# Two 32-head attentions with a gate on one core: the last head joined to the last tile of the output projection, and the first segment's projection units moved to other steps

## The chip, the cores and the metric

The kernel runs on one core of one Trainium2 chip. A core has five engines with a queue each: PE (TensorE, matrix products; its weight loads are listed as PEld), DVE (VectorE), ACT (ScalarE), POOL (GpSimd) and SP (SyncE, which here only issues DMAs). Matmuls write to PSUM; DVE and ACT read it. The metric is the device time of one execution in microseconds (us), lower is better. The kernel before took 2798.84, 2795.10 and 2796.87 us in three runs; the median is 2796.87 us.

## What is computed

Two multi-head attentions over the same 2048 tokens with 32 heads of width 18 each, mixed by a gate. Attention A has its own keys and values for every head, attention B shares one key and value head. All is float32.

```python
def attention_A(x, wqkv, wo):              # S=2048, D=576, H=32, Dh=18
    q, k, v = heads(x @ wqkv)
    p = softmax(q @ k.T * Dh ** -0.5)
    return merge(p @ v) @ wo
def attention_B(x, wq, wk, wv, wo):        # one k and one v for all heads
    q, k, v = heads(x @ wq), x @ wk, x @ wv
    p = softmax(q @ k.T * Dh ** -0.5)
    return merge(p @ v) @ wo

x = A_x
g = sigmoid((x * gate_w).sum(-1, keepdims=True))
out = g * attention_A(x, ...) + (1 - g) * attention_B(x, ...)
```

## The kernel before

**Heads and steps.** The 64 heads (B's 32 first, then A's 32) are called `u` = 0 to 63 (`NU` = 64). After the input projections (phase 1, up to about 290 us), one loop (line 616) runs over `T` in steps of two: every step handles two of the 16 key tiles of one head, so a head takes eight steps and `T // 16` is the head. For every key tile PE makes the scores against all 2048 queries (`step_scores`, four matmuls of 512 columns, line 376), ACT takes their exponential (line 383), and PE multiplies by the values (`step_pv`, line 390), which adds up one head in the single PSUM bank `acc`: 18 rows of output and one row of sums for each of four query chunks.

**Maxima.** The softmax subtracts a row maximum. A second set of score matmuls (`step_max`, line 341), which runs ahead by `LEAD` = 22, that is `M = T + 22`, gives tiles `pm` in PSUM; DVE reduces them (line 350). When `M` is a multiple of 16, so at `T` mod 16 = 10, `max_rows` (line 353) folds the maxima of a whole head, splits them on POOL and sends them through DRAM into two rows of the next query tile. For the last 22 positions there are no maxima left (`alone`); these steps are called ALONE here.

**A head's end.** At `T` mod 16 = 0 `head_out` (line 398) copies `acc` to SBUF on DVE and sends the head's 18 rows for each query chunk to a tile `ot` (row 18u of the merged heads, 128 rows to a tile) and the sums to DRAM. When the tile's last head is done, `normalise(t)` (line 416) loads the sums, takes reciprocals, multiplies by the gate, broadcasts them to a tile `R` and multiplies `ot` by it; the product is split into a rounded part and a remainder (`split`, line 112) and stored in `on_d`.

**The output projection** has 1152 rows: nine tiles of 128, of which the ninth has 110 rows without the last head. It runs in three segments (`SEG`, line 598): tiles 0 to 3, tiles 4 to 7, and the 110 rows. `out_proj` (line 476) is a generator; each `next` makes one *unit*: one of 16 row tiles `st_` of the output and one of two halves of 288 columns. A unit has three products (`PRODS`) for each of its tiles, so 12 matmuls of 288 columns in the first two segments and 3 in the third (line 506), and then an addition into `oacc` in SBUF: by ACT as a copy in the first segment (line 512), by DVE in the others (line 514). Which step makes a unit is set by `due` (line 604): 32 units spread evenly over `T` = 521 to 857, 942 to 1008, and 1021 to 1034. The loop ends with the step at `T` = 1024, so 12 units of the third segment are made inside it and 20 after it.

**The order of a step** is a string (lines 611 to 614): `s` a pair of scores, `m` maxima, `P`, `h`, `H`, `Q` value products (`h` and `H` by halves of 256 columns, `Q` whole), `U` a unit. A step with a unit follows `UNIT`, another one `PLAIN`, the ALONE steps `ALONE`.

```python
PLAIN = "sA0 mA2 sA1 mA0 sA2 mA3 P sA3 mB0 sB0 mB1 sB1 mB2 h sB2 mB3 sB3 x H"
UNIT = "sA0 mA2 sA1 mA0 sA2 mA3 P sA3 mB0 sB0 mB1 sB1 mB2 U sB2 mB3 sB3 x Q"
ALONE = "sA0 sA1 P U sA2 sA3 U sB0 sB1 h U sB2 sB3 H U"
```

**The end.** `normalise(8, at_end=True)` runs at `T` = 1010 on DVE and leaves its two parts in SBUF (`L["end"]`, line 443) in place of two tiles that are free by then. The last head has a path of its own: `prep_last` (line 518) loads its 18 rows of `wo`, and `last_out` (line 533) copies `acc` (line 535), splits it, puts the parts into 54 rows of a query tile with 12 DMAs, and transposes the copy (line 547) to have the sums by rows; `pull(10 ** 9)` then makes the 20 units that are left, and 32 matmuls (line 557) with 32 DVE operations (line 560: the product times the reciprocal sum and gate, plus `oacc`) follow, each second one with the DMA of an output tile (line 562).

Buffers that matter: four PSUM banks for `pm` (maxima, units), three for `ps` (scores), one for `acc`. Every engine works its queue in the order of the program.

Of the kernel before, what the change touches and what calls it, by code (L numbers as in the profile page):

```python
# [8 lines left out]
F32 = mybir.dt.float32  # L9
F32R = mybir.dt.float32r  # L10
# [32 lines left out]
def gated_mix_kernel(ctx: ExitStack, tc: tile.TileContext, xT, wall, wv, wo, out):  # L43
# [351 lines left out]

    OT = {}

    def head_out(u):
        oe = L["work"].tile([P, 512], F32, name="oe", bufs=1)
        nc.vector.tensor_copy(oe, acc)  # L400
        r0 = DH * u
        while r0 < DH * (u + 1):
            t, p = divmod(r0, P)
            n = min(P - p, DH * (u + 1) - r0)
            if t not in OT:
                OT[t] = L["work"].tile([P, S], F32, name="ot")
            for j in range(4):
                s0 = 32 * j + r0 - DH * u
                dma(OT[t][p:p + n, 512 * j:512 * j + 512], oe[s0:s0 + n, :])
            r0 += n  # L410
        dma(sum_d[u].rearrange("(j f) -> j f", j=4), oe[18:128:32, :])
# [4 lines left out]
    def normalise(t, at_end=False):  # L416

        u0 = 0 if t == 0 else last_head(t - 1) + 1
        u1 = min(last_head(t) + 1, NU - 1)
        rows = min(P, DH * (NU - 1) - P * t)  # L420
        n = (u1 - u0) * 16
        sm = L["work"].tile([P, P], F32, name="sm", bufs=1)
        dma(sm[:n, :], sum_d[u0:u1, :].rearrange("h (s f) -> (h s) f", f=P))
        gt = L["work"].tile([P, P], F32, name="gt", bufs=1)
        dma(gt[:n, :], gu_d[u0:u1, :].rearrange("h (s f) -> (h s) f", f=P))
        yield
        yield
        nc.vector.reciprocal(sm[:n, :], sm[:n, :])
        (nc.vector if at_end else nc.gpsimd).tensor_tensor(sm[:n, :], sm[:n, :], gt[:n, :], op=OP.mult)
        yield  # L430
        dma(r_d[u0:u1, :].rearrange("h (s f) -> (h s) f", f=P), sm[:n, :])
        yield
        ot = OT.pop(t)
        R = L["work"].tile([P, S], F32, name="R", bufs=1)
        r0 = P * t
        while r0 < P * t + rows:
            u = r0 // DH
            n = min(DH * (u + 1), P * t + rows) - r0
            dma(R[r0 - P * t:r0 - P * t + n, :], r_d[u:u + 1, :].to_broadcast([n, S]))
            r0 += n  # L440
        yield
        if at_end:
            L["end"] = {"h": qs[1], "l": L["ks"][2]}
            for c in range(4):
                cs = slice(512 * c, 512 * c + 512)
                nc.vector.tensor_tensor(ot[:rows, cs], ot[:rows, cs], R[:rows, cs], op=OP.mult)
                split(ot[:rows, cs], L["end"]["h"][:rows, cs], L["end"]["l"][:rows, cs], nc.vector, nc.vector)
            return
        for c in range(4):
            cs = slice(512 * c, 512 * c + 512)  # L450
            h = L["work"].tile([P, 512], F32R, name="oh", bufs=1)
            l = L["work"].tile([P, 512], F32R, name="ol", bufs=1)
            nc.gpsimd.tensor_tensor(ot[:rows, cs], ot[:rows, cs], R[:rows, cs], op=OP.mult)
            yield
            split(ot[:rows, cs], h[:rows], l[:rows], nc.gpsimd, nc.gpsimd)
            yield
            yield
            dma(on_d[0][P * t:P * t + rows, cs], h[:rows])
            dma(on_d[1][P * t:P * t + rows, cs], l[:rows])
            yield  # L460
# [3 lines left out]
    def prep_wo(t0, rows):  # L464
        nt = len(rows)
        w = {y: L["pool"].tile([P, nt, D], F32R, name=f"wo{y}", tag=f"wo{y}{nt}") for y in "hl"}
        for i, r in enumerate(rows):
            t = t0 + i
            st = L["pool"].tile([P, D], F32, name="wost")
            dma(st[:r], wo[P * t:P * t + r, :])  # L470
            yield
            split(st[:r], w["h"][:r, i, :], w["l"][:r, i, :], nc.gpsimd, nc.gpsimd)
            yield
        WO[t0] = w

    def out_proj(t0, rows, first=False):
# [18 lines left out]
        for q in range(8):  # L495
            if q < 7:
                load(q + 1)
            o = {y: O[q, y] for y in "hl"}
            for s2 in range(2):
                st_ = 2 * q + s2  # L500
                for hf in range(2):
                    fp = ps_m.tile([P, 512], F32, name="pm")
                    n = 0
                    for a, b in PRODS:
                        for t, r in enumerate(rows):
                            nc.tensor.matmul(fp[:, 0:288], o[b][:r, t, s2 * P:(s2 + 1) * P],  # L506
                                             w[a][:r, t, 288 * hf:288 * hf + 288],
                                             start=(n == 0), stop=(n == 3 * nt - 1))
                            n += 1
                    dst = oacc[:, st_, 288 * hf:288 * hf + 288]  # L510
                    if first:
                        nc.scalar.activation(dst, fp[:, 0:288], AF.Copy)
                    else:
                        nc.vector.tensor_tensor(dst, fp[:, 0:288], dst, op=OP.add)  # L514
                    yield


    def prep_last():
        p2 = L["pool"]
        r0 = DH * (NU - 1)  # L520
        st = p2.tile([64, D], F32, name="wlst", tag="wost")
        L["wl"] = p2.tile([64, D], F32R, name="wl")
        l = p2.tile([64, D], F32R, name="wll", tag="wlst2")
        for i in range(3):
            dma(st[18 * i:18 * i + 18, :], wo[r0:r0 + 18, :])
        L["g"] = p2.tile([P, 16], F32, name="gl")
        dma(L["g"], g_d[1].rearrange("(s p) -> p s", p=P))
        yield
        split(st[:54], L["wl"][:54], l[:54], nc.gpsimd, nc.gpsimd)
        yield  # L530
        dma(L["wl"][18:36, :], l[18:36, :])

    def last_out():
        oe = L["work"].tile([P, 512], F32, name="oe", bufs=1)
        nc.scalar.activation(oe, acc, AF.Copy)
        oh = L["work"].tile([P, 512], F32R, name="oh", bufs=1)
        ol = L["work"].tile([P, 512], F32R, name="ol", bufs=1)
        split(oe, oh, ol, nc.scalar, nc.vector)
        stk = qs[2]
        for j in range(4):  # L540
            cs = slice(512 * j, 512 * j + 512)
            dma(stk[0:18, cs], oh[32 * j:32 * j + 18, :])
            dma(stk[18:36, cs], oh[32 * j:32 * j + 18, :])
            dma(stk[36:54, cs], ol[32 * j:32 * j + 18, :])
        pt = ps_m.tile([P, 512], F32, name="pm")
        for c in range(4):
            nc.tensor.transpose(pt[:, P * c:P * c + P], oe[:, P * c:P * c + P], ident)
        r = L["work"].tile([P, 16], F32, name="rl")
        nc.vector.reciprocal(r.rearrange("p (j c) -> p c j", c=4),
                             pt.rearrange("p (c j d) -> p c j d", c=4, d=32)[:, :, :, 18])  # L550
        nc.vector.tensor_tensor(r, r, L["g"], op=OP.mult)
        oacc = L["oacc"]
        yield
        for st_ in range(16):
            for hf in range(2):
                ps = ps_m.tile([P, 512], F32, name="pm")
                nc.tensor.matmul(ps[:, 0:288], stk[0:54, st_ * P:st_ * P + P],
                                 L["wl"][0:54, 288 * hf:288 * hf + 288], start=True, stop=True)
                dst = oacc[:, st_, 288 * hf:288 * hf + 288]
                nc.vector.scalar_tensor_tensor(dst, ps[:, 0:288], r[:, st_:st_ + 1], dst,  # L560
                                               op0=OP.mult, op1=OP.add)
            dma(out[st_ * P:(st_ + 1) * P, :], oacc[:, st_, :])


    NSTEP = 16 * NU
# [12 lines left out]
    def when(T, f):  # L578
        at.setdefault(T, []).append(f)
# [15 lines left out]
    for t in range(8):  # L595
        when(16 * (last_head(t) + 1) + 3, lambda t=t: slow.append(normalise(t)))
    when(16 * (NU - 1) + 2, lambda: run(normalise(8, at_end=True)))
    SEG = ((0, [P] * 4, 450, 521, 857), (4, [P] * 4, 862, 942, 1008), (8, [DH * (NU - 1) - 8 * P], 950, 1021, 1034))
    for t0, rows, Ta, Tb, Tc in SEG:
        when(Ta, lambda t0=t0, rows=rows: slow.append(prep_wo(t0, rows)))  # L600
        when(Tb - 4, lambda t0=t0, rows=rows: (todo.append(out_proj(t0, rows, first=t0 == 0)), pull(1)))
    when(980, lambda: slow.append(prep_last()))

    def due(T, t0, t1, n):
        return (n * (T - t0 + 1)) // (t1 - t0) - (n * (T - t0)) // (t1 - t0) if t0 <= T < t1 else 0

    vunits = [(st_, hf) for hf in range(2) for st_ in range(16)]
# [46 lines left out]
                        slow.pop(0)  # L654
    while slow:
        run(slow.pop(0))
    tail = last_out()
    next(tail)
    pull(10 ** 9)
    run(tail)  # L660


# [32 lines left out]
```

## Time and profile before

| what | time or value |
| --- | --- |
| median of three runs | 2796.87 us |
| the profiled execution | 2797.98 us |
| its span, first to last instruction | 2795.9 us |
| mean granted TensorE clock | 0.995 |
| PE busy in the span | 2767.0 us (99%) |
| DVE, ACT, POOL busy | 2431.6, 2430.6, 207.2 us |
| score matmuls (line 376), share of the chain that ended last | 40% |
| value products (line 390) | 38% |
| units of the output projection (line 506) | 4% |

The span is that of one execution, recorded by the hardware profiler. A matmul's end is modelled, so PE counts as busy almost everywhere, and how long a step takes is read from the starts of its matmuls. The chain that ended last is followed back from the last instruction, at each step to what released it. The granted clock is the share of TensorE's full speed that its throttle let through. Line numbers are those of the kernel before.

### The profile page before, as it was taken

The page shows a single profiled execution, that of the slowest core. Times are in us where ns is not written, and L with a number is a line of the kernel's source. Part 1 is how long each engine was busy: PE and PEld are TensorE (multiplying, and loading weights), DVE is VectorE, ACT ScalarE, POOL GpSimd, SP SyncE. Part 2 cuts the span into 40 slices and gives each one's busy share as a digit, 9 for nine tenths or more (in the row PEclk, how much of TensorE's full clock was granted, in tenths as well). Part 3 has the DMA queues.
Part 4 walks back from the last instruction along what each step waited for, and adds up shares of the span by engine and source line. Part 5 has one row for each costly group of instructions (what it writes and reads, how often), then busy time and mean ns, then how long its engine had stood idle before and what let it go on. Part 6 is the DMA issues. An engine that isn't in the chain of part 4 may idle for free.

```text
span 2795.9 us, 57640 instructions
## 1 busy us (share of the span) xinstructions
PE 2767.0 (99%) x22140; PEld 1229.2 (44%) x22140; DVE 2431.6 (87%) x4524; ACT 2430.6 (87%) x4768; POOL 207.2 (7%) x364
## 2 busy tenths in 40 slices
PE   7999999999999999999999999999999999999999
PEld 5888433333333333333333444444444443334544
DVE  3346999999999999999999999899898999998865
ACT  3231899999999999999999999999999999998775
POOL 2220000001001000100110001000100011001000
PEclk9999999999999999999999999999999999999999
DMA  8662011111112111211143223232232323233412
GB/s 258 221 230 76 27 33 33 31 47 51 40 26 57 55 32 32 64 47 26 45 101 106 70 74 104 61 85 76 80 84 76 79 71 84 63 95 107 103 36 92
DMA packets 137143, 215.09 MB, mean 77 GB/s; under 512 B 55437, under 2 KB 94301, under 8 KB 125182
## 3 DMA queue, kind: packets, MB, share of 16 engines
q1 hardware_dynamic: 116156, 168.13, 22.6%
q10 hardware_dynamic: 14120, 22.30, 2.2%
q0 software_dynamic: 6592, 20.99, 2.2%
q8 instruction: 174, 2.85, 0.4%
q14 instruction: 101, 0.83, 0.1%
HBM read 137.31 MB, written 64.77 MB: 72 GB/s over the span
## 4 chain that ended last, share of the span: by engine, by line
PE 94%; DMA 3%; DVE 2%; issue 0%; SPq 0%; ACT 0%; POOL 0%; DVEq 0%; ACTq 0%; POOLq 0%
PE ps L376 40%; PE acc L390 38%; PE ps L147 5%; PE pm L341 5%; PE pm L506 4%; PE ps L187 2%; DVE mx L350 1%; DMA xs<-xT 1%; DVE oacc L560 0%; DMA qkl<-pl 0%; SPq L49 0%; DMA ksb<-qkl 0%; DMA qs<-qkh 0%; DMA ksa<-qkh 0%; DVE oacc L514 0%
## 5 line engine op out<-in xcount | busy, mean ns | idle before, releaser
L383 ACT ACTIVATE pt<-ps 128x512 f32<-128x512 f32 x4052 | 2128.6, 612 | 108.2 <-PE pm L341 45.6
L350 DVE TENSOR_REDUCE mx<-pm 128x1 f32<-128x512 f32 x3096 | 1975.9, 683 | 168.0 <-PE pm L341 126.7
L376 PE MATMUL ps<-qs,ksb 56*128 56x512 f32 x2688 | 908.2, 437 | 0.0
L341 PE MATMUL pm<-ksb,qs 54*128 54x512 f32 x2364 | 825.5, 446 | 1.1 <-DVE mx L350 0.3
L376 PEld LDWEIGHTS ps<-qs,ksb 56*128 56x128 f32 x2688 | 437.0, 184 | 685.2 <-ACT pt L383 665.1
L390 PE MATMUL acc<-pt,vb 128*19 128x256 f32 (+1 forms) x6144 | 592.5, 457 | 0.1
L390 PE MATMUL acc<-pt,vg 128*19 128x256 f32 (+1 forms) x5656 | 579.3, 481 | 0.7 <-DVE oe L400 0.4
L376 PE MATMUL ps<-qs,ksa 56*128 56x512 f32 x1364 | 455.7, 437 | 0.0
L341 PE MATMUL pm<-ksa,qs 54*128 54x512 f32 x1232 | 433.5, 443 | 0.0
L341 PEld LDWEIGHTS pm<-ksb,qs 54*128 54x128 f32 x2364 | 379.5, 184 | 10.6 <-DVE mx L350 4.1
L376 PEld LDWEIGHTS ps<-qs,ksa 56*128 56x128 f32 x1364 | 218.2, 184 | 342.9 <-ACT pt L383 316.8
L347 DVE CUSTOM_DVE_ANT_0 junk<-pm,xb 128x512 bf16<-128x512 f32 x500 | 339.9, 680 | 0.0
L344 ACT ACTIVATE xb<-pm 128x512 f32<-128x512 f32 x500 | 305.1, 610 | 0.0
L341 PEld LDWEIGHTS pm<-ksa,qs 54*128 54x128 f32 x1232 | 200.3, 184 | 0.9
L390 PEld LDWEIGHTS acc<-pt,vb 128*19 128x19 f32 x6144 | 104.2, 97 | 209.9 <-issue 199.9
L390 PEld LDWEIGHTS acc<-pt,vg 128*19 128x19 f32 x5656 | 95.9, 97 | 209.0 <-issue 197.7
L341 PE MATMUL pm<-kdb,qs 54*128 54x512 f32 x372 | 148.6, 400 | 0.0
L116 POOL CAST mh<-mt 128x32 fp32r<-128x32 f32 x64 | 13.4, 209 | 1683.4 <-DVE mt L358 1683.4
L156 DVE TENSOR_TENSOR pl<-ps,ph 128x512 fp32r<-128x512 f32 x56 | 38.4, 690 | 98.1 <-ACT ph L150 70.2
L150 ACT ACTIVATE ph<-ps 128x512 fp32r<-128x512 f32 x56 | 33.4, 597 | 102.4 <-PE ps L147 87.4
L147 PE MATMUL ps<-xh,wh 128*128 128x512 f32 x280 | 75.6, 401 | 20.9 <-ACT xh L210 13.4
L147 PE MATMUL ps<-xh,wl 128*128 128x512 f32 x280 | 73.5, 393 | 0.0
(99 smaller groups left out, 1334.7 us busy)
## 6 DMA issues: line engine op xcount, KB each, us to landing
qs<-qkh SPq DMA_DIRECT2D x244, 144.0 KB
qs<-qkl SPq DMA_DIRECT2D x122, 144.0 KB
qkh<-ph ACTq DMA_DIRECT2D x56, 256.0 KB
qkl<-pl POOLq DMA_DIRECT2D x56, 256.0 KB, 3.1
ksa<-qkh SPq DMA_DIRECT2D x88, 144.0 KB
onh<-oh SPq DMA_DIRECT2D x32, 256.0 KB
onl<-ol SPq DMA_DIRECT2D x32, 256.0 KB
oih<-onh SPq DMA_DIRECT2D x16, 512.0 KB
```

Of the source, the lines that this page charges most:

```text
L147: nc.tensor.matmul(fp, w[a][:kr, k, :], X[b][:kr, k, cs], start=(n == 0), stop=(n == len(PROJ) - 1))
L150: nc.scalar.activation(h, fp, AF.Copy)
L156: nc.vector.tensor_tensor(l, fp, h.bitcast(F32), op=OP.subtract)
L187: nc.tensor.matmul(fp[:, 0:288], X[b][:kr, k, st_ * P:(st_ + 1) * P], w[a][:kr, k, :], start=(n == 0), stop=(n == len(PROJ) - 1))
L341: nc.tensor.matmul(pm, qs[u % 3][b:b + 54, i * P:(i + 1) * P], k, start=True, stop=True)
L344: nc.scalar.activation(MX["x", u, i], pm, AF.Relu)
L347: nc.vector.tensor_tensor_reduce(junk, pm, MX.pop(("x", u, i)), 1.0, -3e38, op0=OP.add, op1=OP.max, accum_out=MX[u][:, i, c:c + 1])
L350: nc.vector.tensor_reduce(MX[u][:, i, c:c + 1], pm, axis=AX.X, op=OP.max)
L376: nc.tensor.matmul(ps, kst(u)[b:b + 56, i * P:(i + 1) * P], qs[u % 3][b:b + 56, c * 512:(c + 1) * 512], start=True, stop=True)
L383: nc.scalar.activation(pt, ps, AF.Exp, scale=SCALE)
L390: nc.tensor.matmul(acc[32 * j:32 * j + 19, a:b], v_of(u, i), PT[u, i, j][:, a:b], start=(i == 0), stop=(i == 15), skip_group_check=True)
L506: nc.tensor.matmul(fp[:, 0:288], o[b][:r, t, s2 * P:(s2 + 1) * P], w[a][:r, t, 288 * hf:288 * hf + 288], start=(n == 0), stop=(n == 3 * nt ...
```

## The change

Two things are changed.

**The last head.** The tile of 110 rows becomes one of 128: the last head takes rows 0 to 17 and the rest moves up by 18 (`FIRST_ROW`). `last_out` and `prep_last` are gone, and the third segment is no longer in `SEG`: none of its units lies in the loop. After the loop `last_sums` copies `acc` on ACT, transposes it in four blocks, multiplies each query's 18 values by its gate over its sum on DVE, transposes back in 16 blocks, and splits the result (ACT and DVE) into rows 0 to 17 of `L["end"]`. Then all 32 units follow, each with three matmuls over 128 rows. Of their 32 additions four are an ACT copy with an addition on POOL, the others are on DVE; after each second one the output tile's DMA is issued. `keep_busy` puts matmuls with a result that nobody reads between the stages of `last_sums`. Two POOL memsets clear rows 0 to 31 of `ot` (tile 8) and `R`.

**The first segment.** Its 32 units are no longer spread evenly over `T` = 521 to 857. 21 of them are made in the steps `T` = 522, 538, ..., 842 (`T` mod 16 = 10, the steps with `max_rows`) and 11 in the steps `T` = 544, 576, ..., 864 (`T` mod 16 = 0, a head's end), one in each.

```diff
--- before.py
+++ after.py
@@ -395,6 +395,8 @@
 
     OT = {}
 
+    FIRST_ROW = [0] * 8 + [DH]
+
     def head_out(u):
         oe = L["work"].tile([P, 512], F32, name="oe", bufs=1)
         nc.vector.tensor_copy(oe, acc)
@@ -404,6 +406,9 @@
             n = min(P - p, DH * (u + 1) - r0)
             if t not in OT:
                 OT[t] = L["work"].tile([P, S], F32, name="ot")
+                if t == 8:
+                    nc.gpsimd.memset(OT[t][0:32, :], 0.0)
+            p += FIRST_ROW[t]
             for j in range(4):
                 s0 = 32 * j + r0 - DH * u
                 dma(OT[t][p:p + n, 512 * j:512 * j + 512], oe[s0:s0 + n, :])
@@ -418,6 +423,7 @@
         u0 = 0 if t == 0 else last_head(t - 1) + 1
         u1 = min(last_head(t) + 1, NU - 1)
         rows = min(P, DH * (NU - 1) - P * t)
+        off = FIRST_ROW[t]
         n = (u1 - u0) * 16
         sm = L["work"].tile([P, P], F32, name="sm", bufs=1)
         dma(sm[:n, :], sum_d[u0:u1, :].rearrange("h (s f) -> (h s) f", f=P))
@@ -432,19 +438,21 @@
         yield
         ot = OT.pop(t)
         R = L["work"].tile([P, S], F32, name="R", bufs=1)
+        if off:
+            nc.gpsimd.memset(R[0:32, :], 0.0)
         r0 = P * t
         while r0 < P * t + rows:
             u = r0 // DH
             n = min(DH * (u + 1), P * t + rows) - r0
-            dma(R[r0 - P * t:r0 - P * t + n, :], r_d[u:u + 1, :].to_broadcast([n, S]))
+            dma(R[off + r0 - P * t:off + r0 - P * t + n, :], r_d[u:u + 1, :].to_broadcast([n, S]))
             r0 += n
         yield
         if at_end:
             L["end"] = {"h": qs[1], "l": L["ks"][2]}
             for c in range(4):
                 cs = slice(512 * c, 512 * c + 512)
-                nc.vector.tensor_tensor(ot[:rows, cs], ot[:rows, cs], R[:rows, cs], op=OP.mult)
-                split(ot[:rows, cs], L["end"]["h"][:rows, cs], L["end"]["l"][:rows, cs], nc.vector, nc.vector)
+                nc.vector.tensor_tensor(ot[:, cs], ot[:, cs], R[:, cs], op=OP.mult)
+                split(ot[:, cs], L["end"]["h"][:, cs], L["end"]["l"][:, cs], nc.vector, nc.vector)
             return
         for c in range(4):
             cs = slice(512 * c, 512 * c + 512)
@@ -467,7 +475,9 @@
         for i, r in enumerate(rows):
             t = t0 + i
             st = L["pool"].tile([P, D], F32, name="wost")
-            dma(st[:r], wo[P * t:P * t + r, :])
+            if FIRST_ROW[t]:
+                dma(st[:DH], wo[DH * (NU - 1):DH * NU, :])
+            dma(st[FIRST_ROW[t]:r], wo[P * t:P * t + r - FIRST_ROW[t], :])
             yield
             split(st[:r], w["h"][:r, i, :], w["l"][:r, i, :], nc.gpsimd, nc.gpsimd)
             yield
@@ -510,56 +520,51 @@
                     dst = oacc[:, st_, 288 * hf:288 * hf + 288]
                     if first:
                         nc.scalar.activation(dst, fp[:, 0:288], AF.Copy)
+                    elif "end" in L and hf == 0 and st_ in (2, 5, 8, 11):
+                        tmp = L["work"].tile([P, 288], F32, name="tmp", tag="ol", bufs=1)
+                        nc.scalar.activation(tmp, fp[:, 0:288], AF.Copy)
+                        nc.gpsimd.tensor_tensor(dst, tmp, dst, op=OP.add)
                     else:
                         nc.vector.tensor_tensor(dst, fp[:, 0:288], dst, op=OP.add)
+                    if "end" in L and hf:
+                        dma(out[st_ * P:(st_ + 1) * P, :], oacc[:, st_, :])
                     yield
 
-
-    def prep_last():
-        p2 = L["pool"]
-        r0 = DH * (NU - 1)
-        st = p2.tile([64, D], F32, name="wlst", tag="wost")
-        L["wl"] = p2.tile([64, D], F32R, name="wl")
-        l = p2.tile([64, D], F32R, name="wll", tag="wlst2")
-        for i in range(3):
-            dma(st[18 * i:18 * i + 18, :], wo[r0:r0 + 18, :])
-        L["g"] = p2.tile([P, 16], F32, name="gl")
+    def load_gates():
+        L["g"] = L["pool"].tile([P, 16], F32, name="gl")
         dma(L["g"], g_d[1].rearrange("(s p) -> p s", p=P))
-        yield
-        split(st[:54], L["wl"][:54], l[:54], nc.gpsimd, nc.gpsimd)
-        yield
-        dma(L["wl"][18:36, :], l[18:36, :])
-
-    def last_out():
+
+    def last_sums():
+
+        fill = ps_m.tile([P, 512], F32, name="pm")
+
+        def keep_busy(n):
+            for _ in range(n):
+                nc.tensor.matmul(fill[:, 0:304], ident, vb.rearrange("p k d -> p (k d)"), start=True, stop=True)
+
         oe = L["work"].tile([P, 512], F32, name="oe", bufs=1)
         nc.scalar.activation(oe, acc, AF.Copy)
-        oh = L["work"].tile([P, 512], F32R, name="oh", bufs=1)
-        ol = L["work"].tile([P, 512], F32R, name="ol", bufs=1)
-        split(oe, oh, ol, nc.scalar, nc.vector)
-        stk = qs[2]
-        for j in range(4):
-            cs = slice(512 * j, 512 * j + 512)
-            dma(stk[0:18, cs], oh[32 * j:32 * j + 18, :])
-            dma(stk[18:36, cs], oh[32 * j:32 * j + 18, :])
-            dma(stk[36:54, cs], ol[32 * j:32 * j + 18, :])
+        keep_busy(1)
         pt = ps_m.tile([P, 512], F32, name="pm")
         for c in range(4):
             nc.tensor.transpose(pt[:, P * c:P * c + P], oe[:, P * c:P * c + P], ident)
+        keep_busy(2)
+        pt = pt.rearrange("p (c j d) -> p c j d", c=4, d=32)
         r = L["work"].tile([P, 16], F32, name="rl")
-        nc.vector.reciprocal(r.rearrange("p (j c) -> p c j", c=4),
-                             pt.rearrange("p (c j d) -> p c j d", c=4, d=32)[:, :, :, 18])
+        nc.vector.reciprocal(r.rearrange("p (j c) -> p c j", c=4), pt[:, :, :, DH])
         nc.vector.tensor_tensor(r, r, L["g"], op=OP.mult)
-        oacc = L["oacc"]
-        yield
-        for st_ in range(16):
-            for hf in range(2):
-                ps = ps_m.tile([P, 512], F32, name="pm")
-                nc.tensor.matmul(ps[:, 0:288], stk[0:54, st_ * P:st_ * P + P],
-                                 L["wl"][0:54, 288 * hf:288 * hf + 288], start=True, stop=True)
-                dst = oacc[:, st_, 288 * hf:288 * hf + 288]
-                nc.vector.scalar_tensor_tensor(dst, ps[:, 0:288], r[:, st_:st_ + 1], dst,
-                                               op0=OP.mult, op1=OP.add)
-            dma(out[st_ * P:(st_ + 1) * P, :], oacc[:, st_, :])
+        on = L["work"].tile([P, 16, 32], F32, name="on", tag="oh", bufs=1)
+        for c in range(4):
+            nc.vector.tensor_tensor(on[:, c:16:4, 0:DH], pt[:, c, :, 0:DH],
+                                    r[:, c:16:4].unsqueeze(2).to_broadcast([P, 4, DH]), op=OP.mult)
+        for j in range(4):
+            if j == 3:
+                keep_busy(1)
+            cs = slice(512 * j, 512 * j + 512)
+            ps = ps_s.tile([P, 512], F32, name="ps")
+            for c in range(4):
+                nc.tensor.transpose(ps[0:DH, P * c:P * c + P], on[:, 4 * j + c, 0:DH], ident)
+            split(ps[0:DH, :], L["end"]["h"][0:DH, cs], L["end"]["l"][0:DH, cs], nc.scalar, nc.vector)
 
 
     NSTEP = 16 * NU
@@ -595,13 +600,20 @@
     for t in range(8):
         when(16 * (last_head(t) + 1) + 3, lambda t=t: slow.append(normalise(t)))
     when(16 * (NU - 1) + 2, lambda: run(normalise(8, at_end=True)))
-    SEG = ((0, [P] * 4, 450, 521, 857), (4, [P] * 4, 862, 942, 1008), (8, [DH * (NU - 1) - 8 * P], 950, 1021, 1034))
+    SEG = ((0, [P] * 4, 450, 521, 857), (4, [P] * 4, 862, 942, 1008))
     for t0, rows, Ta, Tb, Tc in SEG:
         when(Ta, lambda t0=t0, rows=rows: slow.append(prep_wo(t0, rows)))
         when(Tb - 4, lambda t0=t0, rows=rows: (todo.append(out_proj(t0, rows, first=t0 == 0)), pull(1)))
-    when(980, lambda: slow.append(prep_last()))
+    when(950, lambda: slow.append(prep_wo(8, [P])))
+    when(980, load_gates)
+
+
+    at_rows = list(range(522, 843, 16)) + list(range(544, 865, 32))
+    assert len(at_rows) == 32
 
     def due(T, t0, t1, n):
+        if t0 == SEG[0][3]:
+            return at_rows.count(T)
         return (n * (T - t0 + 1)) // (t1 - t0) - (n * (T - t0)) // (t1 - t0) if t0 <= T < t1 else 0
 
     vunits = [(st_, hf) for hf in range(2) for st_ in range(16)]
@@ -654,10 +666,8 @@
                         slow.pop(0)
     while slow:
         run(slow.pop(0))
-    tail = last_out()
-    next(tail)
-    pull(10 ** 9)
-    run(tail)
+    last_sums()
+    run(out_proj(8, [P]))
 
 
 # ---- launch: one core; inputs and outputs as the reference has them ----
```

## The prediction, made before the result was known

> **What bounds the kernel now.** I read the page first. PE is busy all the time and heads the chain that ended last with 94%.
>
> ```profile
> PE 2767.0 (99%) x22140; PEld 1229.2 (44%) x22140; DVE 2431.6 (87%) x4524; ACT 2430.6 (87%) x4768; POOL 207.2 (7%) x364
> ```
>
> A matmul's end is modelled, so 99% proves little; the price of a unit has to come from step lengths. Then the busy time by stretches of the end, cut at the starts of the last steps (start:end, length, busy and count of PE, PEld, DVE, ACT, POOL, clock, DMA share, GB/s):
>
> ```profile
> 2749.41:2753.33 3.92, 3.92 (x36) 1.25 (x33) 0.75 (x2) 3.92 (x9) 0.00 (x0) 1.00 0.17 42
> 2753.33:2758.34 5.01, 5.01 (x43) 2.02 (x40) 4.84 (x9) 4.52 (x10) 0.00 (x0) 1.00 0.02 5
> 2758.34:2764.99 6.65, 6.65 (x52) 3.28 (x48) 3.77 (x9) 5.05 (x10) 0.00 (x0) 1.00 0.00 0
> 2764.99:2768.74 3.75, 3.75 (x35) 1.73 (x34) 1.87 (x5) 0.00 (x0) 0.00 (x0) 1.00 0.00 0
> 2778.73:2792.41 13.68, 12.36 (x31) 7.14 (x29) 13.68 (x33) 0.00 (x0) 0.00 (x0) 0.67 0.83 307
> ```
>
> An ALONE step without units lasts 3.92 us, with two units 5.01, with five 6.65: a unit of three matmuls adds about 0.55 us there, so it is not free beside ACT. The value products end at 2768.74. In the last row DVE is full and PE waits for it. The timeline shows the tail:
>
> ```profile
> 2768.80 0.60 ACT L535 ACTIVATE oe<-acc 128x512 f32<-128x512 f32 x1 [4.12 <-PE acc L390]
> ...
> 2770.77 0.25 DVE L549 RECIPROCAL rl<-pm 128x16 f32<-128x16 f32 x1
> 2771.05 0.17 DVE L551 TENSOR_TENSOR rl<-rl,gl 128x16 f32<-128x16 f32 x1
> 2771.15 7.67 DVE L514 TENSOR_TENSOR oacc<-pm,oacc 128x288 f32<-128x288 f32 x20
> 2778.25 13.13 PE L557 MATMUL pm<-wl,qs 54*128 54x288 f32 x32
> 2778.73 13.68 DVE L560 SCALAR_TENSOR_TENSOR oacc<-pm,rl,oacc 128x288 f32<-128x288 f32 x32
> 2779.69 13.08 SPq L49 DMA_DIRECT2D out<-oacc  x16
> ```
>
> Between the end of the products and the last DVE operation (2792.41) lie 23.67 us; DMA landing and the program's end add 3.47 more. The 20 units before 2778 run at 0.400 us each, PE's pace; the 32 last operations at 0.427, DVE's. For the first segment I take PE's timeline around a unit in a step with maxima:
>
> ```profile
> 1856.92 0.50 PE L376 MATMUL ps<-qs,ksa 56*128 56x512 f32 x1
> ...
> 1859.70 0.80 PE L506 MATMUL pm<-woh,oih 128*128 128x288 f32 x4
> 1860.34 0.69 PE L506 MATMUL pm<-woh,oil 128*128 128x288 f32 x4
> 1860.87 0.69 PE L506 MATMUL pm<-wol,oih 128*128 128x288 f32 x4
> 1861.49 0.50 PE L376 MATMUL ps<-qs,ksa 56*128 56x512 f32 x1
> ...
> 1863.14 0.50 PE L376 MATMUL ps<-qs,ksa 56*128 56x512 f32 x1
> ```
>
> This step lasts 6.22 us; the same step of a head without a unit 4.56.
>
> **Part 1, units out of the ALONE steps.** Ten units lie before the last value product. Without them the last two score steps start at 2753.33 and 2757.25 and the products of the last step at 2761.17 (two lengths of 3.92). Their three groups take 0.98, 0.55 and 0.63 us, so PE could end at 2763.3. But the second group needs the last exponentials, which end 5.33 us after a step's start in the step at 2749.41, so at 2762.6; the products then end at 2763.8. I take 2763.8, which is 4.9 us earlier; ends 4.4 and 5.4.
>
> **Part 2, the tail from the end of the products (0).** ACT's copy ends at 0.66 and the four transposes at 1.42, as now (2769.40 to 2770.16). Reciprocal and multiply end at 1.96 (0.28 and 0.17 us with their gaps). Four DVE products of 72 elements are new; the nearest row is a PSUM copy of 128x72 at 0.22, so with overlap 0.70 in all (0.5 to 0.9): 2.66. Four transposes back, 0.117 apart and 0.27 long as in the transposes now, end at 3.4; ACT's split, 0.60 for 512 columns, at 4.06; DVE's subtract, 0.69, at 4.8. PE makes the second and third group meanwhile. The fourth waits for a `ps` bank, so for that subtract, and 32 units can start at 5.3. DVE subtracts the other three groups until 6.9, when the first addition starts; four `pm` banks hold four units, and the fifth waits to 7.4 (0.5 lost). 27 more at 0.400 end at 18.8; DVE, 0.37 to 0.38 for an addition, keeps up, the more as four go to ACT and POOL. The last addition ends at 19.3 against 23.67 now: 4.4 us earlier; ends 3.4 (every hand-over of the chain 0.1 us longer) and 5.0.
>
> The matmuls of `keep_busy` (304 columns in four passes, about 0.51 us, by the 0.43 us of 256 columns in the value products) lie under the copy, under the DVE products and under the wait for the fourth bank. If that cover were gone, all four would cost 2.0 us.
>
> **The output DMAs.** 288 KB each now start every 0.85 us with 0.93 of the DMA engines busy (the stretch 2783.28 to 2786.69). Every 0.80 us makes 0.99, so a queue of 0 to 1.0 us may build: +0.3.
>
> **Hidden.** The 12 DMAs of the old last head and its POOL split go, and nobody waited there but this tail. The `ot` memset comes when POOL is idle (2445.9 to 2478.4 holds that head's end), the `R` memset when POOL has nothing left; SP waits some 2.4 us for either (POOL's 0.61 us for a copy of 512 columns, times four); `R` lands at 2752.5 now and the units that need it start at about 2769.
>
> **Part 3, the first segment.** From all step starts between `T` = 520 and 862 I took, for each position in a head, the median step without a unit, and for each unit what its step and the next have above that. At `T` mod 16 = 0, 2, ..., 14 a unit costs 1.570, 1.562, 1.584, 1.644, 1.441, 1.596, 1.583 and 1.591 us, four units each; the even spread sums to 50.3. 21 x 1.596 + 11 x 1.570 is 50.8: +0.5. The only cheap place is 8, where a step without a unit is 0.2 us longer than others (4.83), and the new places leave it out. Ends: -4.2 if all cost 1.441, +1.8 if all cost 1.644 (one of the four with maxima cost 1.662, beside its loads of the next 256 rows; most new ones with such loads lie there).
>
> **Sum.** -4.9 - 4.4 + 0.3 + 0.5 = -8.5 us. The profiled execution, 2797.98 us (span 2795.9 and 2.1 around it), becomes 2789.5; it is 1.1 above the median of the runs shown, so in their terms 2788.4.
>
> **Rivals.** *The clock halves once in the new tail.* The granted clock fell to half three times, at 69.69, 291.55 and 2783.28, twice for 6.83 us; before each lies a stretch of 3.41 us with few matmuls.
>
> ```profile
> 66.28:69.69 3.41, 0.61 (x3) 0.19 (x1) 0.00 (x0) 1.20 (x2) 0.00 (x0) 1.00 0.92 345
> 2776.46:2779.87 3.41, 3.35 (x20) 2.57 (x19) 3.41 (x9) 0.00 (x0) 0.00 (x0) 1.00 0.18 43
> 2779.87:2783.28 3.41, 3.18 (x9) 1.47 (x9) 3.41 (x9) 0.00 (x0) 0.00 (x0) 1.00 0.79 291
> 2783.28:2786.69 3.41, 3.41 (x9) 2.19 (x9) 3.41 (x9) 0.00 (x0) 0.00 (x0) 0.50 0.93 349
> ```
>
> Nine matmuls of 0.133 us (35% of the stretch) were too few, twenty (78%) enough, and so were seven of 512 columns, 0.21 us each (44%), from 45.80 to 49.21. The worst new stretch, 2.2 to 5.6 after the products, has twelve transposes (1.4 us), one `keep_busy` (0.5) and 0.3 of units: 65%, but 24% if transposes do not count for the throttle. Only four large transposes are in the trace, so it cannot say. At half the clock a unit takes 0.80; 6.83 us so lose up to 3.4, some 2.9 as they start before the units: 2791.3.
> The Trainium skill, "TensorE: Matmul & The Clock Gate", Part 1, gives a free-running window of 3413 ns, and the three falls here do lie on such a grid. Its Part 4 says that a transpose doesn't count as PE-busy in the same way, which speaks against this tail: by that rule the sum would be 2791.3 whenever the grid falls badly, else 2788.4.
>
> *The half clock stays to the end,* as it did after 2783.28. Units at 0.80 add 12.8: 2801.2, slower than before. It decides from 21 units at half speed on (8.5 / 0.4). Against it: the two falls followed by dense matmuls ended after 6.83 us, and units are dense.
>
> *The ALONE steps do not get shorter,* because ACT, full in the row of 3.92, sets them: 2793.3. Against it: ACT has 0.5 to 1.6 us of idle time in the steps with units, so these were PE's.
>
> *Units beside maxima or a head's end hide a stall there,* 1.44 each: 2783.7. Against it: the eight such units in the trace.
>
> **Chances.** 0.2% (5.6 us) is about what can be told from no change. Forecast 0.60 (2788.4; a few hundredths reach past 2791.3), one fall of the clock 0.20 (half each side of 2791.3), ALONE unchanged 0.06 (same), stall hidden 0.08 (faster), half clock to the end 0.06 (half same, half slower). Faster 0.76, same 0.21, slower 0.03. The range, 2785.3 to 2793.5, takes in one fall, unchanged ALONE steps and most of the ends of parts 1 to 3, and leaves out the half clock to the end and the hidden stall (0.14).
>
> **What would show it.** After: the products' last matmul 4 to 5 us earlier relative to the last score step; units at 0.400 from about 5.3 us after it; last addition at 19.3; PEclk 1.00 throughout; steps with units at 6.2 to 6.3 us. Units at 0.80, or a chain of `last_sums` well over 5.3 us, would make me wrong.

## The result, and the profile after

The changed kernel takes 2788.22 us (median of 8 runs, 2786.99 to 2789.70) against 2797.05 for the kernel before (8 runs, 2795.10 to 2798.84): a ratio of 0.9968, 95% interval 0.9960 to 0.9977, so 0.32% faster. The profiled execution took 2789.11 us with a span of 2787.2.

The busy times on the page of the changed kernel:

```profile
PE 2758.0 (99%) x22132; PEld 1226.1 (44%) x22132; DVE 2419.9 (87%) x4495; ACT 2433.3 (87%) x4775; POOL 211.9 (8%) x368
```

PE is busy 9 us less and the span is 8.7 us shorter; DVE has 12 us less to do, ACT and POOL 3 to 5 more. The stretches of the end of the changed kernel, cut at step starts, at the end of the value products (2762.61), at the first unit (2767.23) and at the last addition (2781.24); start:end, length, then busy time and count of PE, PEld, DVE, ACT and POOL, clock, DMA share, GB/s:

```profile
2748.34:2752.26 3.92, 3.92 (x37) 1.26 (x34) 0.72 (x2) 3.92 (x9) 0.00 (x0) 1.00 0.24 59
2752.26:2756.19 3.93, 3.93 (x38) 1.26 (x34) 3.79 (x7) 3.93 (x9) 0.00 (x0) 1.00 0.03 6
2756.19:2762.61 6.42, 6.42 (x61) 2.31 (x57) 2.46 (x5) 5.33 (x11) 0.00 (x0) 1.00 0.00 0
2762.61:2767.23 4.62, 4.62 (x28) 2.91 (x29) 2.18 (x8) 2.14 (x4) 0.00 (x0) 1.00 0.00 0
2767.23:2781.24 14.01, 13.34 (x99) 12.87 (x96) 12.79 (x31) 2.23 (x5) 3.23 (x4) 1.00 0.74 280
2781.24:2787.17 5.93, 0.00 (x0) 0.00 (x0) 0.00 (x0) 0.00 (x0) 0.00 (x0) 0.85 0.35 136
```

The step at 2752.26, which in the kernel before held two units and took 5.01 us, takes 3.93. The chain of `last_sums` takes 4.62 us, the units with their additions 14.01, at a full clock. The last row has grown: 5.93 us lie between the last addition and the end, where the kernel before had 3.47. The timeline of the tail:

```profile
2762.65 0.60 ACT L546 ACTIVATE oe<-acc 128x512 f32<-128x512 f32 x1 [1.13 <-PE acc L390]
...
2763.99 0.26 DVE L554 RECIPROCAL rl<-pm 128x16 f32<-128x16 f32 x1 [5.23 <-PE pm L550]
2764.28 0.17 DVE L555 TENSOR_TENSOR rl<-rl,gl 128x16 f32<-128x16 f32 x1
2764.49 0.65 DVE L558 TENSOR_TENSOR on<-pm,rl 128x72 f32<-128x72 f32 x4
...
2766.13 2.68 DVE L118 TENSOR_TENSOR ksb<-ps,qs 18x512 fp32r<-18x512 f32 x4 [0.99 <-ACT qs L114]
...
2768.74 3.68 DVE L528 TENSOR_TENSOR oacc<-pm,oacc 128x288 f32<-128x288 f32 x9
2769.57 12.03 SPq L49 DMA_DIRECT2D out<-oacc  x16
```

What fills the 5.93 us is not in a row of busy time, because draining an engine counts as sequencer work. The instructions of the program's last line tell it (engine, operation, count: shortest/median/longest in ns, first and last start in us); here those of POOL and SP, first of the kernel before, then of the changed one:

```profile
L691 POOLq DRAIN  x3: 40/102/8139, 2713.8 to 2795.6; - x3
L691 SPq DRAIN  x3: 7/7/7, 2795.0 to 2795.4; - x3
```

```profile
L701 POOLq DRAIN  x3: 40/102/8696, 2777.7 to 2786.9; - x3
L701 SPq DRAIN  x3: 7/7/7, 2784.4 to 2786.6; - x3
```

At the end of the program every engine drains and then all meet. SP drains once the output DMAs have landed: at 2784.44 in the changed kernel. POOL's long DRAIN begins at 2777.7 and lasts 8.70 us, to 2786.39, and the meeting waits for it. It ends 7.85 us after POOL's last addition (2778.54). In the kernel before the same 7.85 us (2714.13 to 2721.98) lay far ahead of the end.

Where the time went, stage by stage, from the two traces (each from the first score matmul of a step, or the end of the value products):

| stage | before | changed | difference |
| --- | --- | --- | --- |
| start to `T` = 512 | 1478.45 | 1477.40 | -1.05 |
| `T` = 512 to 880 (first segment) | 905.90 | 905.84 | -0.06 |
| `T` = 880 to 1008 | 345.28 | 345.33 | +0.05 |
| `T` = 1008 to the end of the products | 39.11 | 34.05 | -5.06 |
| end of the products to the last addition | 23.68 | 18.63 | -5.05 |
| last addition to SP's DRAIN | 2.63 | 3.20 | +0.57 |
| SP's DRAIN to the end | 0.83 | 2.73 | +1.90 |

The first row lies ahead of everything that was changed. In thirteen traces of this work `T` = 512 began between 1475.56 and 1479.17 us, so 1.05 us there is scatter of one execution against another, and the median of a few runs can be off by one or two for the same reason. The other rows repeat far better, and the readings below go by them. They sum to -7.65 us.

### The profile page after: what moved, and what is told of

It is laid out like the page before. It is cut to its first block, busy times and chain, and to the rows that moved or that the text cites. A ratio compares the mean times of both kernels' runs of the same rounds, so it can differ in the third digit from the quotient of the medians.

```text
span 2787.2 us, 57590 instructions
## 1 busy us (share of the span) xinstructions
PE 2758.0 (99%) x22132; PEld 1226.1 (44%) x22132; DVE 2419.9 (87%) x4495; ACT 2433.3 (87%) x4775; POOL 211.9 (8%) x368
## 4 chain that ended last, share of the span: by engine, by line
PE 97%; DMA 2%; DVE 1%; SPq 0%; issue 0%; ACT 0%; POOL 0%; POOLq 0%; DVEq 0%
PE ps L376 41%; PE acc L390 38%; PE ps L147 5%; PE pm L341 5%; PE pm L516 4%; PE ps L187 2%; DMA qkl<-pl 0%; DMA ksb<-qkh 0%; DMA xs<-xT 0%; DMA wst<-wall 0%; SPq L49 0%; DVE mx L350 0%; PE pm L376 0%; DMA qkh<-ph 0%; DVE oacc L528 0%
```

## The experiments

Theory: the tail gains as the prediction says, and POOL's drain gives 1.9 us of it back. Main rival: the late landing of the output DMAs sets the end, and the drain waits beside it. Ratios are to the kernel before.

**The four POOL additions.** On DVE, earlier, or later:

```diff
-                    elif "end" in L and hf == 0 and st_ in (2, 5, 8, 11):
+                    elif False:                                                  # e1_adds_dve
+                    elif "end" in L and hf == 0 and st_ in (1, 3, 5, 7):         # e2_pool_early
+                    elif "end" in L and hf == 0 and st_ in (2, 5, 8, 14):        # e3_pool_late
```

> All 32 additions of the tail on DVE, none on POOL. In the changed kernel POOL's DRAIN ends 7.85 us after POOL's last addition (2778.54 to 2786.39), 1.9 us after SP has seen the last output DMA land. Theory (this drain sets the end): POOL's last work is then the memset of R some 70 us earlier, the end follows the last landing, and the kernel is 1.9 us faster than the changed one (2786.3 if that is 2788.2); DVE has 32 additions of 0.38 us where PE makes a unit every 0.40, so it keeps up. Rival 1 (the late landing of the output DMAs sets the end and the drain only waits beside it): 0. Rival 2 (DVE needs the relief of the four additions): 1 us slower or more.

> The four POOL additions are those of row tiles 1, 3, 5 and 7 in place of 2, 5, 8 and 11, so POOL's last one comes four row tiles, 3.2 us, earlier. Theory (the drain sets the end): its end falls at about 2783.2 on the changed kernel's time axis, before the last landing at 2784.0, so 1.9 us faster than the changed kernel, as with no POOL at all. Rival 1 (landings set the end): 0. Rival 2 (DVE needs relief): the same as the theory here, so this run and e1_adds_dve differ by a us or more.

> The last of the four POOL additions moves from row tile 11 to row tile 14, three row tiles or 2.4 us later. Theory (POOL's drain of 7.85 us after its last addition sets the end): 2.4 us slower than the changed kernel, about 2790.6. Rival 1 (landings set the end): 0, or at most the 0.8 us by which that row tile's DMA is issued later.

| | median us (runs) | ratio, 95% interval | products' end to last addition | to SP's DRAIN | to the end | in all |
| --- | --- | --- | --- | --- | --- | --- |
| changed | 2788.22 (8) | 0.9968, 0.9960 to 0.9977 | 18.63 | 3.20 | 2.73 | 24.56 |
| e1_adds_dve | 2786.92 (5) | 0.9964, 0.9952 to 0.9977 | 18.67 | 3.27 | 0.83 | 22.77 |
| e2_pool_early | 2787.73 (5) | 0.9965, 0.9952 to 0.9979 | 18.62 | 3.81 | 0.84 | 23.27 |
| e3_pool_late | 2793.45 (11) | 0.9984, 0.9975 to 0.9993 | 18.66 | 3.31 | 5.00 | 26.96 |

The same rows of the last line, of e1_adds_dve and then of e3_pool_late, whose last POOL addition ends at 2782.97:

```profile
L701 POOLq DRAIN  x3: 40/102/9874, 2712.2 to 2784.5; - x3
L701 SPq DRAIN  x3: 7/7/7, 2783.9 to 2784.3; - x3
```

```profile
2782.17 0.80 POOL L526 TENSOR_TENSOR oacc<-tmp,oacc 128x288 f32<-128x288 f32 x1 [4.00 <-ACT tmp L525]
```

```profile
L701 POOLq DRAIN  x3: 40/102/8691, 2782.1 to 2791.3; - x3
L701 SPq DRAIN  x3: 7/7/7, 2786.6 to 2791.1; - x3
```

Moving the last addition by +2.4 us moves the end by +2.40 us in the trace (26.96 against 24.56); taking POOL out, or far enough forward, gives 1.79 and 1.29 us and leaves 0.83 and 0.84 us behind SP's DRAIN, as in the kernel before. (With POOL's additions earlier the outputs land 0.5 us later than without POOL; why was not tried.) The rival, landings alone, would have left all three alike. The times lean the same way, but the medians of the first two lie within the scatter of the changed kernel's, so the traces decide. For e3_pool_late the median is 5.2 us above the changed kernel's, where 2.4 was expected, and its runs scatter most, from 2789.14 to 2796.09. Of the 4.4 us by which its trace is longer 1.77 lie ahead of `T` = 512; what makes the runs scatter so was not found. DVE loses nothing by 32 additions (18.67 against 18.63), so the relief that POOL gave was not needed.

**The output DMAs.** As e1_adds_dve, with half of the output left out:

```diff
-                    if "end" in L and hf:
+                    if "end" in L and hf and st_ % 2:
```

> As e1_adds_dve (no POOL in the tail), but only the output tiles of odd row tiles are sent to DRAM, so half of the output is left out; the additions are all made. In the changed kernel SP passes its wait for the output DMAs 3.2 us after the last addition, in the variants 3.3 to 3.8, in the kernel before 2.63. Theory (16 tiles of 288 KB at one per 0.80 us are about what the DMA engines can write, and a queue builds up): with half the tiles the last one finds no queue, 2.6 us. Rival (the transfer is slower for another reason, such as the engines' own traffic): 3.2 us or more.

The median is 2785.97 us (3 runs, 0.9962, 0.9947 to 0.9977). From the last addition to SP's DRAIN it took 2.57 us, as the queue theory said. The stretch from 2777.00 to 2780.50 in this kernel, and below it the one in the changed kernel (the last two columns are DMA share and GB/s):

```profile
2777.00:2780.50 3.50, 3.05 (x23) 2.82 (x22) 3.50 (x9) 0.00 (x0) 0.00 (x0) 1.00 0.53 203
```

```profile
2777.00:2780.50 3.50, 3.50 (x29) 3.50 (x27) 3.16 (x9) 0.41 (x1) 0.81 (x1) 1.00 1.01 385
```

With all tiles the DMA engines are full (1.01), with half of them at 0.53. So the tail now ends on a queue of output DMAs, worth 0.5 to 1.3 us in the traces with all tiles at this pace (3.20 to 3.87, against 2.57 here and 2.63 and 2.66 in the two kernels whose tiles come every 0.85 us).

**The fill matmuls.** `keep_busy` left out:

```diff
-            for _ in range(n):
+            for _ in range(0):
```

> The four matmuls of keep_busy, whose result nobody reads, are left out. Theory (transposes count for the throttle about as matmuls do, the 16 back and the 4 forth make 1.9 us of work in the worst stretch of 3.41 us, 55%): the clock stays at 1.00 until the units are done and the time is that of the changed kernel within 0.5 us. Rival (transposes do not count): no counted work for 4.6 us, a fall of the clock in every execution, units at 0.80 us in 6.83 us of it, 2.5 to 3.4 us slower.

The median is 2789.93 us (7 runs, 0.9973, 0.9962 to 0.9984); the tail of its one trace is the same, 24.55 us, and the clock does not fall in it. On the grid of the throttle (the falls start at multiples of 3.41 us from each other) the first row below is the stretch with the fewest matmuls that are not transposes, and the second the one behind it:

```profile
2765.80:2769.21 3.41, 2.60 (x21) 1.99 (x22) 2.42 (x7) 1.94 (x4) 0.00 (x0) 1.00 0.00 0
2769.21:2772.63 3.42, 3.25 (x24) 3.01 (x23) 3.23 (x9) 0.61 (x2) 0.81 (x1) 1.00 0.27 100
```

Of the 21 matmuls in the first row 16 are transposes and 5 are of units: 5 x 0.133 is 20% of 3.41 us, and yet the next stretch runs at 1.00. In the trace of e8_both (below) a stretch with ten matmuls of the same units and no transpose was followed by half the clock:

```profile
2776.12:2779.53 3.41, 1.26 (x10) 1.03 (x8) 1.76 (x5) 0.00 (x0) 0.00 (x0) 1.00 1.02 389
2779.53:2782.40 2.87, 0.00 (x0) 0.00 (x0) 0.00 (x0) 0.00 (x0) 0.00 (x0) 0.50 0.30 113
```

So transposes count here. The Trainium skill ("TensorE: Matmul & The Clock Gate", Part 4) says that a transpose doesn't count as PE-busy in the same way; the measurement decides against that rule for this tail. The profile lists these transposes as plain matmuls, so it does not tell whether they run in the mode that the Trainium skill means. The window of 3413 ns that the Trainium skill gives (same page, Part 1) agrees with the traces: the falls ahead of the tail are 3.41, 6.83, 10.24 or 13.65 us long, one to four windows.

The bounds by share of time that the prediction took (35% too few, 44% enough) do not hold in general. The fall at 291.55 in the kernel before follows this stretch, with 13 matmuls of 512 columns in it:

```profile
288.14:291.55 3.41, 2.81 (x13) 1.03 (x11) 3.41 (x7) 2.80 (x6) 0.00 (x0) 1.00 0.06 19
```

Those matmuls have 54 or 56 of the 128 rows. An estimate from the records of all thirteen traces, from 30 us on: sum rows times columns of the matmuls that start in a stretch of the grid, transposes included. Below 340 thousand all 41 stretches were followed by a fall, from 390 to 459 thousand 7 of 19, above that none of more than 10,000. The first row above has 184 thousand without its transposes and 446 thousand with them. No run changed the rows alone, so this is a pattern and not a shown cause.

By this count the tail without fills lies where some stretches were followed by a fall, and the grid lies elsewhere in each execution. So the fills bring nothing in this trace, and whether they do in other executions stays open. The median is 1.7 us above the changed kernel's; the trace is 1.3 us longer, 0.73 ahead of `T` = 512 and 0.50 from there to `T` = 880, with nothing in the tail.

**The placement of the first segment's units.** Spread evenly again (run twice, the second time beside the changed kernel itself), and with the 21 units of the maxima steps one step earlier, at `T` mod 16 = 8:

```diff
     def due(T, t0, t1, n):
-        if t0 == SEG[0][3]:                                   # e5_first_tail, e11_even
-            return at_rows.count(T)
...
-    at_rows = list(range(522, 843, 16)) + list(range(544, 865, 32))
+    at_rows = list(range(536, 857, 16)) + list(range(544, 865, 32))    # e6_units_at_8
```

> The changed kernel with the first segment's units spread evenly over T = 521 to 857 as before: the change of the tail alone. From the first score matmul of T = 512 to that of T = 880 the kernel before took 905.90 us and the changed one 905.84. Theory (a unit costs 1.57 to 1.59 us wherever it lies, but for one place): 905.9 here too, and the time of the changed kernel within 0.5 us. Rival 1 (the sum of the prediction): 0.5 us faster than the changed kernel. Rival 2 (the new places hide a stall at the maxima or a head's end): a us or more slower.

> The changed kernel with the 21 units at T mod 16 = 10 moved to T mod 16 = 8 (T = 536, 552, ..., 856); the 11 at a head's end stay. In the trace of before four units there cost 1.441 us each, and a step there without a unit is 0.2 us longer than others. Theory (the unit fills a gap of PE that is there in every head): the stretch from T = 512 to 880 falls by 21 x (1.587 - 1.441) = 3.1 us to 902.8, the time to 2785.1. Rival (those four were cheap because of what lay beside them): 905.8, and no difference to the changed kernel.

> The changed kernel itself once more, for comparison with the next one on the same chip and with a second trace. 905.8 to 906.1 us from T = 512 to 880, 24.6 us from the end of the value products to the end, and 2788.2 with a scatter of the median of about a us, because the start of T = 512 alone lay between 1475.6 and 1479.2 us in ten traces.

> e5_first_tail once more (units of the first segment spread evenly, the rest as changed). Its median was 2790.35, 2.1 us above the changed kernel's, with a trace that differs by 0.2 us. Theory (the placement is worth nothing, the 2.1 us are scatter of the part before it): within 1 us of e10_changed, stretch 906.0. Rival (the placement saves 2 us that one trace did not show): again 2 us above e10_changed, and its stretch at 907 or more.

| | median us (runs) | ratio, 95% interval | `T` = 512 to 880 |
| --- | --- | --- | --- |
| changed | 2788.22 (8) | 0.9968, 0.9960 to 0.9977 | 905.84 |
| e10_changed | 2788.29 (6) | 0.9968, 0.9956 to 0.9979 | 905.94 |
| e5_first_tail | 2790.35 (10) | 0.9978, 0.9969 to 0.9987 | 906.01 |
| e11_even | 2788.86 (8) | 0.9973, 0.9962 to 0.9984 | 905.96 |
| e6_units_at_8 | 2786.26 (5) | 0.9963, 0.9950 to 0.9975 | 902.58 |

The even spread costs 905.90, 906.01 and 905.96 us in three traces, the new placement 905.84 and 905.94 (and 905.75 to 906.34 in the other variants that have it): the second part of the change is worth nothing. The 2.1 us between the medians of e5_first_tail and the changed kernel shrank to 0.6 when both ran side by side, and the stretch of the placement differs by no more than 0.2, so they are scatter. Position 8 is another matter. PE's rows at the start of `T` = 512 and of `T` = 880, of the changed kernel and then of e6_units_at_8:

```profile
1477.40 0.50 PE L376 MATMUL ps<-qs,ksa 56*128 56x512 f32 x1
...
2383.24 0.49 PE L376 MATMUL ps<-qs,ksb 56*128 56x512 f32 x1
```

```profile
1477.86 0.50 PE L376 MATMUL ps<-qs,ksa 56*128 56x512 f32 x1
...
2380.44 0.49 PE L376 MATMUL ps<-qs,ksb 56*128 56x512 f32 x1
```

905.84 against 902.58: 3.26 us less, where the four units of the old trace had promised 3.1. Every head has a gap of PE at that position (its step is 0.2 us longer than others), and a unit there fills most of it. The traces show what PE waits for: in all 22 steps of the changed kernel at this position between `T` = 520 and 862 the weight load of the last maxima matmul (line 341) starts at least 0.10 us late, by the semaphores in 19 of them because DVE has yet to reduce the tile in its bank (line 350); in the 21 that have a unit in e6_units_at_8 it does not wait. Why DVE is behind just there was not tried.

**The two halves of the gain.** The kernel before with the third segment's units all behind the loop:

```diff
     def due(T, t0, t1, n):
+        if t0 == 1021:
+            return 0
         return (n * (T - t0 + 1)) // (t1 - t0) - (n * (T - t0)) // (t1 - t0) if t0 <= T < t1 else 0
```

> The kernel before, with one edit: none of the third segment's 32 units is made in the loop, all of them after it; the last head keeps its own path with 32 matmuls and DVE operations. Theory (a unit costs about 0.5 us in the ALONE steps and 0.40 after them): from the first score matmul of T = 1008 to the end of the value products 34.05 us as in the changed kernel (39.11 before), 4.0 us more of units behind it, so 1.1 us faster than before, 2796; the rest of the gain comes from the 32 operations that the joined tile saves. Rival (taking the units out of the loop is what gains, the joined tile is about even): 4 to 5 us faster than before.

2795.93 us (11 runs), 0.9998 (0.9989 to 1.0007): no difference. Its stretches, cut at `T` = 1008, at the end of the products, the last unit and the last addition:

```profile
2728.32:2762.36 34.04, 33.66 (x284) 10.86 (x280) 8.90 (x15) 32.88 (x67) 0.00 (x0) 1.00 0.15 37
2762.36:2776.78 14.42, 13.73 (x102) 13.42 (x101) 12.99 (x34) 1.23 (x2) 0.00 (x0) 1.00 0.13 32
2776.78:2790.87 14.09, 12.93 (x32) 8.18 (x32) 14.09 (x34) 0.00 (x0) 0.00 (x0) 0.58 0.78 293
```

The loop's end is 5.06 us shorter, as in the changed kernel, and the tail 4.85 us longer (31.99 against 27.14): units only change places, at 0.40 us outside for 0.5 inside, and PE now waits for the copy of `acc` without units to fill the time. I had expected 1.1 us of gain; the 0.9 us that is missing is that wait (`acc` ends at 2762.36, the first unit starts at 2763.46). The real gain is the third row, 14.09 us, nearly all of it the 32 DVE operations for the last head, which the joined tile does without; in its place stands the chain of `last_sums`, 4.62 us. From this kernel to the changed one, with the same end of the loop, the joined tile shortens what lies behind the products from 31.99 to 24.56 us in the traces, the wait for POOL's drain included.

**Both findings together.** All additions on DVE and the 21 units at position 8:

> The changed kernel with both edits that its trace points to: all 32 additions of the tail on DVE (as in e1_adds_dve) and the 21 units at T mod 16 = 8 (as in e6_units_at_8). Theory (the two costs are independent): 1.8 and 3.1 us, together 4.9 us faster than the changed kernel, 2783.3. Rival (the cheap place is not there in number): 1.8 us, 2786.4.

2783.78 us (5 runs, 2782.53 to 2784.45), 0.9954 (0.9940 to 0.9968): faster than the kernel before by 0.46%, and 4.4 us below the changed one. In the trace the first segment takes 902.97 us and the tail 23.19, 4.2 us less than the changed kernel in the two.

## Why the prediction was right

The forecast was 2788.4 us, range 2785.3 to 2793.5; 2788.22 was measured. The place of the gain was right; several terms were off, and the errors partly cancel.

- *Part 1, units out of the ALONE steps:* -4.9 forecast, -5.06 measured. The products of the last step do wait for the last exponentials, and they end 6.42 us after the start of the last score step, where 6.55 was reckoned.
- *Part 2, the tail's chain:* -4.4 forecast, -5.05 measured. Units start 4.62 us after the products in place of 5.3: the transposes back start at 2764.82, while the four DVE products still run (to 2765.14), where the sum put one after the other, so ACT's first split starts 2.90 us after the products in place of 3.4. The start of the additions (6.13, 6.9 reckoned) and the pace of 0.40 us followed.
- *The output DMAs:* +0.3 with ends 0 and 1.0, measured +0.57; e9_half_out shows that it is the queue that was named.
- *Part 3, the placement:* +0.5 forecast, -0.06 measured. The means over four units each were too coarse: the 0.5 us is 0.016 us for each of 32 units. That the new places leave out the only cheap one was right, and e6_units_at_8 gives the price of that, 3.3 us.
- *What failed:* POOL's late work was put at nothing. Part 2 counts the four additions on POOL only as relief for DVE, and the step "Hidden" looks only at who waits for the results of POOL's memsets. The end of the program waits too: POOL's drain, 7.85 us after its last operation, was in the trace of before, ending at 2721.98, and became 1.9 us of the path when POOL was given work 8.6 us before the end.
- *The rivals:* no fall of the clock in the new tail, nor without fills in the one trace of that. The reading that few matmuls lie before each fall is wrong for the second one, which follows 13 of them. ALONE steps did get shorter; a unit beside maxima or a head's end hides no stall. The stall that can be hidden is one step before the maxima.

The sum by stages is -7.65 us against -8.5, the medians differ by 8.83. That the forecast came within 0.2 us is partly luck: a missed cost of 1.9 us stands against terms that gained 0.2 to 0.7 more than reckoned, and the scatter ahead of the changed part adds 1.05 in the two traces.

## What to carry to other kernels

An engine's last instruction has a price of its own: look at where each engine's end-of-program drain ends before giving late work to an engine that had none, above all to POOL, and move such work forward or elsewhere. When work can be placed freely, get its price for every position of a repeating pattern from the starts of its steps; a position whose step is longer than its neighbours takes extra work for less. And split a gain into its halves by an experiment: work that is moved out of a loop comes back behind it unless something else takes it over.

## What the runs showed of the hardware

- POOL's DRAIN at the end of the program ends 7.85 us after its last operation in all thirteen traces (7.848 to 7.851), whether that was an addition of 288 columns, a small subtract or a memset. The longest DRAIN of another engine took 1.11 us.
- Transposes count for the clock: a stretch of 3.41 us with 16 of them and five unit matmuls was followed by a full clock, one with ten unit matmuls and no transpose by half the clock.
- The share of time in which PE is busy does not decide the clock: 2.81 us of matmuls with 54 or 56 rows in a stretch of 3.41 us were followed by a fall, 2.15 us with 128 rows (2778.59 to 2782.00 in the changed kernel) were not.
- With 288 KB every 0.80 us the DMA engines are at 1.01 of their time and 385 GB/s; a queue of 0.5 to 1.3 us forms at the end.
